# A pre-norm attention and gated-FFN block on one core: the first chunk's order, VectorE's share and the judging of batches changed in a planned schedule

## The chip, the cores and the metric

The kernel runs on one core of one Trainium2 chip. The metric is the device time of one execution in microseconds (us). A core has five engines that run side by side and wait for each other through semaphores: PE (TensorE, matrix products; its weight loads are listed apart as PEld), DVE (VectorE), ACT (ScalarE), POOL (GpSimd) and SP (SyncE, which here only issues DMA transfers). Each engine takes its own instructions in the order in which the program has them. Matrix products are written to PSUM, a small memory of eight banks of 2 KB for each of 128 partitions; everything else lives in SBUF.

## The reference

A transformer block on one sequence of 2048 tokens of 512 features, in bf16: layer norm, attention with 32 heads of 16 dimensions, a residual sum, layer norm, a gated FFN with 1792 hidden features, a second residual sum.

```python
def _A_ref(x, wqkv, wo):
    qkv = transpose(reshape(x @ wqkv, (B, S, 3, H, Dh)))     # H = 32, Dh = 16
    q, k, v = qkv[0], qkv[1], qkv[2]
    p = softmax(einsum("bhqd,bhkd->bhqk", q, k) * Dh ** -0.5)
    o = einsum("bhqk,bhkd->bhqd", p, v)
    return reshape(o, (B, S, D)) @ wo

def _B_ref(x, w_gate, w_up, w_down):
    g, u = x @ w_gate, x @ w_up
    return (sigmoid(g) * u) @ w_down

h  = x + _A_ref(layernorm(x), wqkv, wo)
h2 = h + _B_ref(layernorm(h), w_gate, w_up, w_down)
```

The costly part is the exponential of 32 x 2048 x 2048 scores.

## The kernel before, in words

**Units, tiles and groups.** Scores are computed transposed: keys on the partitions, queries along the row. A *unit* is 128 keys by 512 columns for one place `j` of four in a row of the PE array. Three units (`GU = 3`, three PSUM banks, tile `pss`) make a score tile; two such tiles fit, so the scores of tile n wait until both readers of tile n - 2 are done. There are 683 tiles, numbered in the order of their work. A *group* is 64 units. Groups with heads 0 to 7 cover a chunk of 512 queries (`(c, 0)`, `(c, 1)`); the others, `(4 + h, p)`, cover half a chunk, 256 queries of half `h`, with the eight heads of a pair `p` (1 to 3). `gseq` (L807 to 812) lists the 32 groups in their order. `(c, 0)` of all four chunks come first, then for each chunk `(c, 1)` and its six half groups. In the first chunk the halves are interleaved.

**Exponentials on two engines.** Of each score tile ACT takes two or three units in one instruction (`pt`, six buffers; L1421). In a *split* tile, one unit goes to DVE, which approximates the exponential with integer arithmetic: a linear function of the score, written as 16-bit integers and read again as bf16 (tile `J`, L1233), and three further codes that add constants to it (`code`, L1253), four units at a time. Whether tile n is split is decided in `act_step` (L1401 to 1415) by DVE's backlog and the buffers at hand. A tile that is not split is called whole here.

**Values.** PE multiplies `pt`, `J` and the codes with V (`acc`, L1207); V has a column of constants for the sums. A unit on ACT needs one such product, a unit on DVE four. At a group's end DVE transposes `acc` to `xs` (L1145) and inverts the sums, POOL scales (L1111, L1117), and DVE transposes to `ot`.

**Background work.** Everything else on PE stands in a queue `bg` of generators: V for 16 key tiles (`prep_v`, L677), K for each pair (`prep_k`, L689), Q for each chunk and pair (`prep_q`, L746), the output projection with the second layer norm's statistics (`wo_add`), the FFN's up-projections (`ffn_up`) and down-projections (`ffn_down`) for each half. Each has a due tile; `FFN_DUE` (L969) has those of the FFN. K and Q need a chain over several engines: PE projects, DVE scales (`kd` L703, `qd` L762), SP issues eight transfers that spread the rows to four places (`spread`, L194), and a shift of the exponents follows the same way (`kr` L725, `kcol` L731, `sh` L777, its transfers L780). If work that a step needs has not been done, `force` (L1017) puts it in front at once.

**The planner.** The order of each engine's instructions is written out by a planner when the program is built. It keeps a clock per engine (`T`), lets the engine that is furthest behind take the next step (`pe_step`, `act_step`, `dve_step`, `gps_step`), and places instructions by fixed costs. `pe_step` (L1323) takes scores when their two readers will be done; else it picks a batch of ready value units (`pick`, L1344) and chooses between it (`"a"`), background work (`"b"`), an idle product that keeps PE active (`fill`, L653), and waiting 40 ns. `good` (L1349) says whether a batch is full enough. `credit` grows with the rate at which background work falls due.

**Waits of the scores.** For a split tile, `dve_step` notes both readers, the exponential and DVE's first code (L1449), and `scores` (L1064) makes the first product of tile n depend on both of tile n - 2. `ex_end` is the time from which the planner thinks that the scores may start; after DVE's first code it adds 125 ns (L1447).

**The end.** After the last tile the rest of the background work, the last value products, and the FFN of the last half run one after the other.

Of the kernel before, what the change touches and what calls it, by code (L numbers as in the profile page):

```python
# [26 lines left out]
def kernel(  # L27
# [12 lines left out]
    P = 128  # L40
    S, D = A_x.shape[1], A_x.shape[2]
# [8 lines left out]
    NQC = S // QC  # L50
# [757 lines left out]
    for c in range(NQC):  # L808
        gseq += [(c, 1)]
        pairs, both = range(1, NP), (2 * c, 2 * c + 1)  # L810
        gseq += [(NQC + h, p) for h in both for p in pairs] if c else \
            [(NQC + h, p) for h, p in ((0, 1), (1, 1), (0, 2), (0, 3), (1, 2), (1, 3))]

    def chunk_of(q):
        return q if q < NQC else (q - NQC) // 2
# [150 lines left out]

    HOLD = Mark(None)
    LEAD = 12
    FFN_DUE = (256, 326, 395, 464, 533, 603, 672)  # L969
    bg = deque()  # L970
    done = {("q", 0, 0, 0), ("v0", 0)}

# [75 lines left out]
    def scores(n):  # L1048
        for k in queries(n):
            force(k)  # L1050
        pss = ps_s.tile([P, GU, QC], FP32, name="pss")
        first = True
        for a in range(2):
            for ui, (q, g, kt, j) in enumerate(tiles[n]):
                hg = head_groups(q, g)
                if a >= len(hg):
                    continue
                w = QC // len(hg)
                mm = nc.tensor.matmul(  # L1059
                    pss[:, ui, a * w:(a + 1) * w],  # L1060
                    lhsT=KT[hg[a]][32 * j:32 * j + 32, kt * P:(kt + 1) * P],
                    rhs=(QT0[q] if q < NQC and g == 0 else QT[hg[a]])[32 * j:32 * j + 32, columns(q, a)],
                    start=True, stop=True, tile_position=(32 * j, 0))
                for r in readers.get(n - 2, ()) if first else ():  # L1064
                    tc.add_manual_dep(mm.ins, r.ins.name,
                                      DependencyInfo(DependencyClass.Sync, DependencyReason.DATA),
                                      reason="both readers of the bank's last scores")
                first = False
        T["P"] = max(T["P"] + switch("s"), ex_end.get(n - 2, -LAT) + LAT, arrived(n)) + SMM
        worked(SMM * 0.25 * len(tiles[n]))  # L1070
        sc_end[n] = T["P"] + 165
        pss_n[n] = pss
# [98 lines left out]
    def av_cost(uns):  # L1171
        return MM * max(sum(un.u[3] == j for un in uns) for j in range(4))
# [147 lines left out]
    credit = 0.0  # L1320
    nxt = {"s": 0, "e": 0}

    def pe_step():  # L1323
        nonlocal credit
        t, s, e = T["P"], nxt["s"], nxt["e"]
        ready = None
        if s < N and (s < 2 or s - 2 in ex_end):
            ready = max(ex_end.get(s - 2, -LAT) + LAT, arrived(s))
            if ready <= t + 100 * (st["mode"] != "s") + 20:
                scores(s)  # L1330
                nxt["s"] += 1
                for q, p, kt, j in tiles[s]:
                    if (q, kt, j) == (NQC + NH - 1, NT - 1, 3):
                        for g in range(2 * p * (p > 1), min(2 * p + 2, FC // 2)):
                            load_pair(late_pair(g), g)
                return
        drop_read()
        last_sc = sc_end.get(e, t + 400.0)
        act_end = max(T["A"], last_sc + LAT if e < s else T["A"])
        limit = act_end + (s - e) * 905 - 520 if s < N else 1e12  # L1340
        room = limit - t
        got = [av_ready(60.0, r) for r in (1, 2, 3, 4)]
        got = [v for v in got if v and S_OUT * (st["mode"] != "a") + av_cost(v) <= room + 100]
        pick = max(got, key=lambda v: len(v) / (100 + av_cost(v))) if got else []  # L1344
        old = min((un.n for un in avq if un.held is None), default=e)
        press = e - old >= NPT - 1 or len(codes) >= CB - PRESS or len(first_codes) >= NJB or e == N
        press = press or st["cur"] < len(gseq) and lasts[gseq[st["cur"]]] < e
        last = 0 < len(pick) == av_left()
        good = pick and len(pick) * MM / 4 >= RATE * (100 + av_cost(pick))  # L1349
        group = tiles[min(e, N - 1)][-1][:2]  # L1350
        floor = -4 if not jq and T["D"] + pending() < t + 300 and lasts[group] - e < 100 else 0
        order = []
        if st["work"] == "b" and st["mode"] != "s" and credit > floor and not (press and pick):
            order.append("b")
        if last or press or good and credit < 2:
            order.append("a")
        if credit > floor:
            order.append("b")
        if good:
            order.append("a")  # L1360
        for kind in order:
            if kind == "a" and pick and av(av_cost(pick) / MM):
                return
            if kind == "b" and (2 * MM + S_OUT * (st["mode"] == "s") <= room + (0 if credit < 8 else 500)):
                used = try_bg(1e9)
                if used:
                    credit -= used
                    return
        free_pm = not st["open"] and (st["pm"] is None or st["pm"].end is not None
                                      and st["pm"].end + LAT <= t)  # L1370
        if FILL and free_pm and active(t) < FILL and MM + S_OUT * (st["mode"] == "s") <= room + FROOM:
            fill()
            return
        T["P"] = t + 40

    def act_step():
# [21 lines left out]
        taken, full = taken[len(taken) // NJ * NJ:], -(-len(taken) // NJ)  # L1398
        held_codes = len(codes) + sum(len(c.ops) for c in chains) + NCODE * full
        pick = None  # L1400
        if (len(tl) == GU and len(jq) < 2  # L1401
                and (not fresh or held_codes + NCODE <= CB and len(first_codes) + full - (len(half) > 0) < NJB)
                and max(T["D"] - start, 0.0) + 600 * len(jq) <= LATE and back <= BACK
                and len(avq) <= QMAX):
            can = [w for w in (GU - 1, 0)
                   if (fresh or tl[w][:2] == taken[0].u[:2])
                   and (back + LAST + (NJ - 1 - len(taken)) * LQ) * LS
                   <= left_in[tl[w][:2]] * 1130 + GEND]
            js = [un.u[3] for un in taken]
            good = [w for w in can if tl[w][3] not in js]  # L1410
            if good:
                pick = good[0]
            elif can and back <= EASY:
                pick = can[0]
# [20 lines left out]
    def dve_step():  # L1435
# [7 lines left out]
        if jq and sc_end[jq[0][0]] + LAT <= t + WAITJ and (half or len(first_codes) < NJB):  # L1443
            n, pss, un, ex = jq.popleft()
            first = dexp_first(pss, un)
            T["D"] = max(t, sc_end[n] + LAT) + 600
            ex_end[n] = max(un.end, T["D"] + 125)  # L1447
            tc.declare_no_dep(first.ins, ex.ins, reason="other banks of the tile")
            readers[n] = (ex, first)  # L1449
            return  # L1450
        if chains and chains[0].group == gseq[st["cur"]] and lasts[chains[0].group] < nxt["e"] + HURRY:
            pop_chain()
# [150 lines left out]
```

## Time and profile before

| | |
|---|---|
| median of 3 runs | 805.17 us (804.78 to 805.35) |
| profiled execution | 804.94 us |
| its span, first to last instruction | 803.2 us |
| mean granted clock of PE | 0.993 of full speed |
| score tiles | 683: 500 split, 182 whole, and the last with two units |

Times in rows are us from the start of the span. A row of the timeline has start, length, engine, line, operation, what it writes and reads, sizes and a count; merged rows run from the first start to the last end. In brackets stands how long the engine was idle before and what ended that. In groups (rows with two bars), the columns are busy time in us and mean duration in ns, then idle time in front. Rows of successive instructions of one engine can overlap, since a record runs from start to end and the next one may start before that end. "PEld" rows are weight loads, and "SPq" rows are the issues of transfers, not the transfers. The trace tells nothing of the planner's own clocks; where instructions stand against each other in the built program is told as "in the order".

### The profile page before, as it was taken

Reading aid. Unit: us, or ns where it says so; the run is one execution under the profiler, and the core shown is the slowest. Engines: PE = TensorE matmul, PEld = TensorE weight load, DVE = VectorE, ACT = ScalarE, POOL = GpSimd, SP = SyncE. Lnnn points to the kernel's source line nnn. Section 1 sums busy time; section 2 is a strip of 40 time slices with the busy share of each in tenths; the row PEclk is TensorE's granted clock in tenths of the full one; section 3 lists DMA queues with packets and bytes.
Section 4 is the critical chain, followed back from the end, with each engine's and each line's share of the span. In section 5 each row is a group of like instructions: output and inputs, shape, how many; then the busy total and the mean of one; then the engine's idle time right before and its main releaser. Section 6 shows DMA issues by size and latency. Waiting matters only on the chain.

```text
span 803.2 us, 34789 instructions
## 1 busy us (share of the span) xinstructions
PE 759.2 (95%) x15324; PEld 369.7 (46%) x15328; DVE 730.0 (91%) x1325; ACT 760.2 (95%) x780; POOL 52.7 (7%) x131
## 2 busy tenths in 40 slices
PE   9899998999888999999999999999999999999998
PEld 7322222443433544455445444564454446545655
DVE  7999998999979999998999998999999989999962
ACT  6999998999999999999999999999999999999962
POOL 4000000000001000100010002000100010010000
PEclk9999999999989999999999999999999999999999
DMA  6403012122400132023102220221113202322600
GB/s 194 120 2 71 2 28 61 28 66 44 151 2 22 36 102 84 10 76 100 44 16 73 77 85 11 75 82 55 36 50 97 72 29 82 108 72 79 174 28 14
DMA packets 91862, 51.32 MB, mean 64 GB/s; under 512 B 21376, under 2 KB 90624, under 8 KB 91712
## 3 DMA queue, kind: packets, MB, share of 16 engines
q1 hardware_dynamic: 91184, 49.03, 22.2%
q8 instruction: 121, 1.98, 1.0%
q14 instruction: 29, 0.24, 0.1%
q10 hardware_dynamic: 528, 0.07, 0.1%
HBM read 39.52 MB, written 2.11 MB: 52 GB/s over the span
## 4 chain that ended last, share of the span: by engine, by line
PE 38%; ACT 30%; DVE 18%; issue 10%; DMA 2%; POOL 1%; SPq 1%; DVEq 0%; ACTq 0%
ACT pt L1421 28%; PE pm L186 12%; PE acc L1207 11%; PE pss L1059 11%; DVE J L1233 8%; DVE code L1253 4%; PE gu L181 2%; ACT th L929 2%; DVE kd L703 1%; DVE xs L1145 1%; PE hp L1568 1%; DMA code<-in_A_x_dram 1%; DVE Vaug L206 1%; DMA k<-kr 1%; DVE sqk L711 0%
## 5 line engine op out<-in xcount | busy, mean ns | idle before, releaser
L1421 ACT ACTIVATE pt<-pss 128x1024 bf16<-128x1024 f32 (+1 forms) x683 | 720.1, 1174 | 11.7 <-PE pss L1059 7.2
L1233 DVE TENSOR_SCALAR J<-pss 128x512 uint16<-128x512 f32 x500 | 330.2, 676 | 22.5 <-PE pss L1059 21.3
L1059 PE MATMUL pss<-QT,KT 32*128 32x256 bf16 (+1 forms) x3584 | 269.8, 290 | 31.4 <-ACT pt L1421 20.2
L1253 DVE TENSOR_SCALAR code<-J 128x2048 uint16<-128x2048 uint16 (+2 forms) x390 | 246.5, 663 | 0.4
L1207 PE MATMUL acc<-pt,Vaug 128*17 128x256 bf16 (+1 forms) x2706 | 226.2, 292 | 1.2 <-DVE xs L1145 0.5
L1059 PEld LDWEIGHTS <-KT 32*128 32x128 bf16 x3584 | 81.7, 92 | 233.3 <-ACT pt L1421 126.4
L1207 PE MATMUL acc<-code,Vaug 128*17 128x256 bf16 (+1 forms) x2634 | 187.8, 289 | 0.2
L1207 PEld LDWEIGHTS <-Vaug 128*17 128x17 bf16 x6218 | 136.6, 90 | 96.2 <-issue 76.3
L1207 PE MATMUL acc<-J,Vaug 128*17 128x256 bf16 (+1 forms) x878 | 140.8, 291 | 0.6 <-DVE Vaug L206 0.4
L186 PE MATMUL pm<-xT,wgu 128*32 128x256 bf16 x3136 | 114.1, 274 | 0.5
L186 PEld LDWEIGHTS <-wgu 128*32 128x32 bf16 x3136 | 76.6, 96 | 25.8 <-issue 22.3
L186 PE MATMUL pm<-wd,hT 128*32 128x512 bf16 x784 | 54.8, 382 | 0.0
L1111 POOL TENSOR_TENSOR o<-xs,rec 128x256 bf16<-128x256 f32 x23 | 17.2, 747 | 421.4 <-DVE rec L1107 421.4
L913 DVE SCALAR_TENSOR_TENSOR hT<-th,pm 128x512 bf16<-128x512 f32 x49 | 32.9, 672 | 7.6 <-PE pm L186 6.8
L929 ACT ACTIVATE th<-pm 128x512 f32<-128x512 f32 x49 | 30.8, 628 | 0.2
L1145 DVE STREAM_TRANSPOSE xs<-acc 128x512 f32<-128x512 f32 x32 | 22.7, 709 | 6.4 <-PE acc L1207 6.3
L186 PEld LDWEIGHTS <-hT 128*32 128x32 bf16 x784 | 15.9, 95 | 19.7 <-issue 12.5
L186 PE MATMUL pm<-xT,wk_sb 128*32 128x512 bf16 x256 | 19.2, 383 | 0.5 <-DVE kd L703 0.5
L186 PE MATMUL pm<-xT,wq_sb 128*32 128x512 bf16 x256 | 19.3, 388 | 0.0
L1117 POOL TENSOR_TENSOR o<-xs,rec 128x256 bf16<-128x256 f32 x8 | 5.6, 705 | 190.0 <-DVE rec L1107 190.0
L186 PE MATMUL pm<-wv_sb,xT 128*32 128x448 bf16 x256 | 17.4, 356 | 0.5 <-DVE Vaug L206 0.5
L186 PE MATMUL pm<-wo_sb,ot 128*32 128x512 bf16 x224 | 16.9, 383 | 0.1
(156 smaller groups left out, 367.8 us busy)
## 6 DMA issues: line engine op xcount, KB each, us to landing
wgu<-in_B_w_gate_dram SPq DMA_DIRECT2D x49, 256.0 KB
wgu<-in_B_w_up_dram SPq DMA_DIRECT2D x49, 256.0 KB
KT<-ones SPq DMA_DIRECT2D x7, 512.0 KB
out_dram<-ob SPq DMA_DIRECT2D x15, 128.0 KB
KT<-kd SPq DMA_DIRECT2D x28, 64.0 KB
QT<-qd SPq DMA_DIRECT2D x112, 16.0 KB
wd<-in_B_w_down_dram SPq DMA_DIRECT2D x1, 1792.0 KB
xr<-in_A_x_dram SPq DMA_DIRECT2D x14, 128.0 KB
```

The costliest lines, as they stand in the source:

```text
L181: nc.tensor.matmul(ps, lhsT=lhsT, rhs=rhs, start=start, stop=stop)
L186: nc.tensor.matmul(ps[r, :], lhsT=lhsT[:, r], rhs=rhs, start=start, stop=stop, tile_position=(0, 32 * j), skip_group_check=True)
L206: nc.vector.tensor_scalar(out=Vaug[:, t, 4:H, 0:DH], in0=ps[:, 0:D - 64].rearrange("p (h d) -> p h d", d=DH), scalar1=rstd[:, t:t + 1], sc ...
L913: nc.vector.scalar_tensor_tensor(out=hT[:, 2 * k:2 * k + 2, :].rearrange("p f q -> p (f q)"), in0=th[:], scalar=1.0, in1=ps, op0=ALU.add, ...
L929: nc.scalar.activation(out=th[:], in_=ps, func=ACT.Tanh, scale=0.5)
L1059: mm = nc.tensor.matmul(pss[:, ui, a * w:(a + 1) * w], lhsT=KT[hg[a]][32 * j:32 * j + 32, kt * P:(kt + 1) * P], rhs=(QT0[q] if q < NQC and ...
L1111: V.tensor_tensor(out=o2[:, 0:NB, :].rearrange("p b (a d) -> p a b d", a=2), in0=xs[:, :, 0:DH].rearrange("p (a b) d -> p a b d", a=2), in ...
L1145: j = st["acc"] = dve(630, lambda: nc.vector.transpose(out=xs[:].rearrange("p b r -> p (b r)"), in_=acc[:]), Mark(T["P"]))
L1207: nc.tensor.matmul(acc[32 * j:32 * j + VW, a * w:(a + 1) * w], lhsT=Vaug[:, kt, 4 * hg[a] + j, :], rhs=un.ap[:, a * w:(a + 1) * w], start= ...
L1233: first = nc.vector.tensor_scalar(out=J[:, k, :], in0=src, scalar1=128 * SC * LOG2E, scalar2=float(CODE_BASE), op0=ALU.mult, op1=ALU.add)
L1253: nc.vector.tensor_scalar(out=c, in0=j, scalar1=CODE_STEP[i], scalar2=None, op0=ALU.add)
L1421: ex = nc.scalar.activation(out=pt[:, lo:lo + wa, :], in_=pss[:, lo:lo + wa, :], func=ACT.Exp, scale=SC)
```

## The change

Six edits:

- In the first chunk, `gseq` takes half 0's three pairs and then half 1's, as in the other chunks.
- The FFN's due tiles begin at 220 instead of 256 and end at 672 as before, evenly spaced.
- In tiles 30 to 139, every third tile may not be split.
- A batch of value units is judged without the 100 ns for a change of the array's mode, unless PE comes from scores; and where PE would otherwise only wait, it takes a batch that is at least 40% full if the next background work isn't ready before the batch is over (`bg_ready` is new).
- The scores of tile n carry a dependence on DVE's first code of tile n - 2 alone; that on the exponential is left to the buffer's own tracking, which puts it on the first product.
- The planner lets the scores start 50 ns after its end of DVE's first code, instead of 125.

```diff
     for c in range(NQC):
         gseq += [(c, 1)]
         pairs, both = range(1, NP), (2 * c, 2 * c + 1)
-        gseq += [(NQC + h, p) for h in both for p in pairs] if c else \
-            [(NQC + h, p) for h, p in ((0, 1), (1, 1), (0, 2), (0, 3), (1, 2), (1, 3))]
+        gseq += [(NQC + h, p) for h in both for p in pairs]
...
-    FFN_DUE = (256, 326, 395, 464, 533, 603, 672)
+    FFN_DUE = (220, 295, 371, 446, 521, 597, 672)
...
-                for r in readers.get(n - 2, ()) if first else ():
-                    tc.add_manual_dep(mm.ins, r.ins.name,
+                if first and n - 2 in readers:
+                    tc.add_manual_dep(mm.ins, readers[n - 2].ins.name,
                                       DependencyInfo(DependencyClass.Sync, DependencyReason.DATA),
-                                      reason="both readers of the bank's last scores")
+                                      reason="VectorE's reading of the bank's last scores")
...
+    def bg_ready():
+        if not bg or bg[0][2] is None or credit <= -4:
+            return 1e12
+        ends = [d.end for d in bg[0][2][2] if d is not None]
+        return T["P"] + 300 if None in ends else max(ends, default=-LAT) + LAT
...
-        pick = max(got, key=lambda v: len(v) / (100 + av_cost(v))) if got else []
+        pick = max(got, key=lambda v: len(v) / (100 * (st["mode"] == "s") + av_cost(v))) if got else []
...
-        good = pick and len(pick) * MM / 4 >= RATE * (100 + av_cost(pick))
+        good = pick and len(pick) * MM / 4 >= RATE * (100 * (st["mode"] == "s") + av_cost(pick))
...
+        if pick and len(pick) * MM / 4 >= .4 * av_cost(pick) and bg_ready() >= t + 1 * (S_OUT * (st["mode"] != "a") + av_cost(pick)):
+            if av(av_cost(pick) / MM):
+                return
         T["P"] = t + 40
...
-        if (len(tl) == GU and len(jq) < 2
+        if (len(tl) == GU and len(jq) < 2 and not (30 <= n < 140 and n % 3 == 0)
...
-            ex_end[n] = max(un.end, T["D"] + 125)
+            ex_end[n] = max(un.end, T["D"] + 50)
             tc.declare_no_dep(first.ins, ex.ins, reason="other banks of the tile")
-            readers[n] = (ex, first)
+            readers[n] = first
```

## The prediction

> **What bounds the kernel now.** I read the page's engine totals and its chain first, then busy time in six equal stretches of attention (110 tiles each, the last 102) with the stretch before them, then the exponentials by form, then the waits and the timeline where ScalarE stood still.
>
> ```profile
> span 803.2 us, 34789 instructions
> PE 759.2 (95%) x15324; PEld 369.7 (46%) x15328; DVE 730.0 (91%) x1325; ACT 760.2 (95%) x780; POOL 52.7 (7%) x131
> ACT pt L1421 28%; PE pm L186 12%; PE acc L1207 11%; PE pss L1059 11%; DVE J L1233 8%; DVE code L1253 4%; PE gu L181 2%; ACT th L929 2%; DVE kd L703 1%; DVE xs L1145 1%; PE hp L1568 1%; DMA code<-in_A_x_dram 1%; DVE Vaug L206 1%; DMA k<-kr 1%; DVE sqk L711 0%
> L929 ACT ACTIVATE th<-pm 128x512 f32<-128x512 f32 x49 | 30.8, 628 | 0.2
> ```
>
> The totals show PE and ACT level, and ACT's exponentials are the chain's largest entry with 28%; the shares alone decide nothing. The stretches do (columns: length, then busy time of PE, PE's weight loads, DVE, ACT, POOL, each with its instructions, then the granted clock and two DMA columns):
>
> ```profile
> 22.20:54.20 32.00, 28.61 (x335) 10.64 (x334) 31.62 (x61) 31.98 (x31) 0.62 (x1) 1.00 0.30 76
> 54.20:175.80 121.60, 112.35 (x1682) 38.35 (x1675) 116.46 (x214) 116.61 (x112) 3.43 (x5) 1.00 0.20 42
> 175.80:295.30 119.50, 109.25 (x2117) 49.30 (x2111) 111.22 (x197) 115.97 (x116) 8.04 (x16) 0.96 0.20 54
> 295.30:415.50 120.20, 117.13 (x2707) 58.39 (x2695) 109.63 (x194) 119.53 (x121) 9.73 (x25) 1.00 0.21 61
> 415.50:536.50 121.00, 116.25 (x2654) 60.26 (x2655) 112.52 (x201) 120.59 (x123) 7.09 (x15) 1.00 0.22 63
> 536.50:655.60 119.10, 116.57 (x2516) 55.79 (x2516) 112.07 (x197) 118.78 (x121) 8.78 (x25) 1.00 0.20 58
> 655.60:769.60 114.00, 110.79 (x2800) 62.37 (x2795) 107.17 (x189) 112.62 (x117) 6.95 (x15) 1.00 0.33 94
> ```
>
> ACT leaves 0.7, 0.4, 0.3 and 1.4 us uncovered in the last four stretches, but 5.0 and 3.5 us in the second and third row, where DVE (116.46 of 121.60) or the clock (0.96) comes in. ACT is the bound; the others matter where they make it late. What one exponential costs, by form and as unbroken runs of five and of four:
>
> ```profile
> L1421 ACT ACTIVATE pt<-pss 128x1024 bf16<-128x1024 f32 x501 | 485.4, 1062 | 10.3 <-PE pss L1059 6.3 <-PE acc L1207 2.9
> L1421 ACT ACTIVATE pt<-pss 128x1536 bf16<-128x1536 f32 x182 | 260.1, 1483 | 1.3 <-PE pss L1059 0.9
> 90.50 4.73 ACT L1421 ACTIVATE pt<-pss 128x1024 bf16<-128x1024 f32 x5
> 38.53 5.48 ACT L1421 ACTIVATE pt<-pss 128x1536 bf16<-128x1536 f32 x4
> ```
>
> A split tile (two units on ACT, one on DVE) comes every (4.73 - 1.06) / 4 = 0.91 us, a whole one every (5.48 - 1.48) / 3 = 1.33: a unit given back to ACT costs 0.42 us. In a run the records overlap by 1.06 - 0.91 = 0.15. At these paces 500 splits, 182 wholes and 49 tanh (30.8) fill 455.0 + 242.1 + 30.8 = 728 of the 747.4 us from 22.2 to 769.6; so ACT is late by about 19 us in all, some 7.6 of it in 54.2 to 175.8 (121.6 - 77 x 0.91 - 33 x 1.33). That is what the change can win.
>
> **The change, part by part.** Sums are against the profiled execution (804.94 us, its span and 1.7 around it), which is 0.2 below the median 805.17. What the planner makes of the edits stands in the order of the two built programs; counts "in the order" are from there.
>
> *Fewer units on VectorE.* In the order 485 tiles are split instead of 500; 12 of the 15 lie in tiles 30 to 139 (45 wholes for 33). ACT gets 15 x 0.42 = **+6.3 us**, on the path. DVE loses 15 first codes, and PE 60 of 6218 value matmuls; both are off the path.
>
> *Halves one by one, and other batches.* Three single places where ACT stood still, each with its cause:
>
> ```profile
> 120.22 4.20 ACT L1421 ACTIVATE pt<-pss 128x1024 bf16<-128x1024 f32 x4 [1.48 <-PE acc L1207]
> 139.42 0.69 DVE L206 TENSOR_SCALAR Vaug<-pm,rstd 128x448 bf16<-128x448 f32 x1 [1.04 <-PE pm L186]
> 140.16 0.11 PEld L1207 LDWEIGHTS <-Vaug 128*17 128x17 bf16 x7 [0.64 <-DVE Vaug L206]
> 141.35 1.02 ACT L1421 ACTIVATE pt<-pss 128x1024 bf16<-128x1024 f32 x1 [1.77 <-PE pss L1059]
> 261.22 1.02 ACT L1421 ACTIVATE pt<-pss 128x1024 bf16<-128x1024 f32 x1 [1.45 <-PE acc L1207]
> ```
>
> At 120.22 and 261.22 the exponential waits for value matmuls that still read its six-deep output buffer: in the order tiles 85 and 213 are last read seven score tiles later. After the change no tile is read later than six, and one at six. At 141.35 PE had to make V tiles 13 to 15 in front of the scores, since the value matmuls already wanted them (the last V step stands at tile 107, and the first of the three is wanted at 105); in the new order the last one stands at tile 100. With the lost overlap the three come to 1.48 + 1.77 + 1.45 + 3 x 0.15 = **-5.2 us**. What is late next at these places is the ordinary lateness, which stays in the sum.
>
> The clock: the last of these three and one more stretch lie where it was halved.
>
> ```profile
> 229.00:231.00 2.00, 1.15 (x24) 0.51 (x18) 0.69 (x1) 2.00 (x3) 0.00 (x0) 1.00 0.04 8
> 231.00:233.00 2.00, 0.92 (x18) 0.24 (x13) 1.42 (x3) 2.00 (x3) 0.00 (x0) 0.89 0.00 0
> 232.50:239.40 6.90, 6.39 (x84) 2.10 (x84) 5.94 (x11) 5.87 (x7) 0.62 (x1) 0.51 0.00 0
> 259.80:263.30 3.50, 3.31 (x56) 1.63 (x60) 3.27 (x8) 2.08 (x3) 0.62 (x1) 0.51 0.02 5
> 113.94 1.07 PE L186 MATMUL pm<-xT,wq_sb 128*32 128x512 bf16 x16
> ```
>
> PE was 46 to 58% busy in the 4 us before 232.5; then ACT lost 1.0 us uncovered, some 1.5 with the overlap. Four 512-column matmuls side by side take (1.07 - 0.38) / 3 = 0.23 us at most (last row); counted at 0.22, the thinnest four tiles of PE work in the order hold 0.27 of ACT's time (tiles 191 to 194, just there) and 0.32 (215, 216, the second episode); after the change the thinnest is 0.35, since half 0 ends at tile 170 instead of 191 and its FFN fills the gap from tile 179 on instead of 207. I take **-1.5 us**; the ends are -1.5 and +3 (two new episodes). The Trainium skill ("TensorE: Matmul & The Clock Gate", Part 1) says that the clock halves after an idle window of about 3.4 us. By that rule nothing in either order halves it, and -1.5 stands; the trace disagrees, as half-busy was enough.
>
> Batches are judged without the 0.1 us for a change of mode unless PE comes from scores, and one is taken in place of idling. In the order 146 stretches between score groups hold four or more rounds of matmuls instead of 174 (16% fewer), and 16 are empty instead of 34, though PE changes its array mode 48 times more. Of the 19 us, 19 - 6.7 = 12.3 remain; 16% of that is **-2.0 us**, between 0 and -4.
>
> *The third wait.* Now 485 score groups begin with a wait instruction for DVE, then a weight load that waits for ACT; after, the load waits for DVE and the first matmul for ACT, and no separate wait instruction is left.
>
> ```profile
> PE pss L1059 <- DVE J L1233: 6.1, 18, 0.9
> 454.11 0.68 DVE L1233 TENSOR_SCALAR J<-pss 128x512 uint16<-128x512 f32 x1
> 454.91 0.13 PEld L1059 LDWEIGHTS <-KT 32*128 32x128 bf16 x3 [0.50 <-ACT pt L1421]
> 454.94 0.39 PE L1059 MATMUL pss<-QT,KT 32*128 32x512 bf16 x3 [0.23 <-DVE J L1233]
> 118.98 0.71 DVE L1145 STREAM_TRANSPOSE xs<-acc 128x512 f32<-128x512 f32 x1
> 119.74 0.38 PE L1207 MATMUL acc<-pt,Vaug 128*17 128x512 bf16 x1 [0.53 <-DVE xs L1145]
> ```
>
> J ends at 454.79 and the matmul starts 0.15 later; a PE instruction with a DVE wait of its own starts 0.05 after it (119.69 to 119.74). So J lets the scores go 0.10 sooner, on 18 waits: -1.8. The planner now counts on it (release 0.75 us after J's start instead of 0.83). If the wait instruction was not the cause, PE stands 0.08 longer before those scores: +1.4. The xs row is the nearest of the same engine, so I take **-1.5**. Who queues behind: everything on PE.
>
> *Moved steps.* Pairs 2 and 3 are needed at tiles 128 and 149 instead of 149 and 170. Their K chain on SP before:
>
> ```profile
> 153.08 0.68 DVE L703 TENSOR_TENSOR kd<-pm,RK 128x512 bf16<-128x512 f32 x1
> 153.79 5.62 SPq L198 DMA_DIRECT2D KT<-kd  x8
> 159.51 2.70 SPq L728 DMA_DIRECT2D k<-kr  x4
> 163.31 0.14 DVE L731 TENSOR_REDUCE kcol<-k 8x1 f32<-8x4 f32 x1 [0.68 <-DMA k<-kr]
> 167.37 1.14 SPq L780 DMA_DIRECT2D QT<-sh  x2
> ```
>
> From kd's end (153.76) to the last of 22 issues (168.51) 14.75 us, and 1.1 for a landing (162.21 to 163.31): 15.9. In the new order kd's last piece stands at tiles 111 and 132, 15 to 16 exponentials before the scores that need it, which is 16.1 to 17.5 us at the paces above. It just fits; before, 30 us lay between. I put **+0.5**, up to +2.4 if both come a microsecond late. The FFN's first weight loads queue on SP behind the last of these issues, as before, at tile 143 instead of 158. POOL's normalisations move with their groups; its rows are 7% busy. The new FFN due times only shift background work, counted in the batches.
>
> *The end.* One up-projection more is left after the last scores: 32 matmuls at 114.1 / 3136 = 0.036 us, **+1.0** with its DVE step covered by the down-projection behind it.
>
> ```profile
> L186 PE MATMUL pm<-xT,wgu 128*32 128x256 bf16 x3136 | 114.1, 274 | 0.5
> ```
>
> Sum: 6.3 - 5.2 - 1.5 - 2.0 - 1.5 + 0.5 + 1.0 = -2.4: 802.5 for a profiled run, **802.7** against the median.
>
> **Rivals.** *The lateness comes back elsewhere* (slower). ACT hands two score buffers to PE, and any order has tiles where PE comes late; if the named stalls are only replaced by others, ACT's 6.3 and the end's 1.0 remain: 812. It decides from where less than 6.2 of the 10.2 us is recovered (then over +1.6). For it: three named stalls of four are one-offs of an order, and the new order was laid out with the same costs. Against: no V step is forced and no buffer is read at seven.
>
> *Two new half-clock episodes or both landings late* (no change): +3 or +2, about 805. The skill's rule speaks against the episodes, the row at 231 for them: the new order has lows of 0.35 to 0.37 at tiles 42, 85, 139 and 321.
>
> *A larger gain*: if DVE, 96% covered in the second row and relieved there of 11 first codes, and the 18 fewer empty stretches take another 4 us of the remaining 10, it is 798.
>
> **How the numbers follow.** 0.2% (1.6 us) is about what a measurement can tell here. Forecast, 800 to 803.5: 0.36; larger gain, below 800: 0.18; no change: 0.18; slower, 807 to 812: 0.28. So faster 0.54, same 0.18, slower 0.28. The range, 797.5 to 810, leaves out the far ends of the larger gain and of the returned lateness; the forecast's own is 800 to 804.
>
> **What would show it.** ACT's long forms go to 197 and the stretch of tiles 30 to 139 to about 114.1 + 5.0 plus 2 to 4 us of lateness; no ACT wait over 1 us for PE's acc or after a Vaug wait; clock 1.00 through attention; scores 0.05 instead of 0.15 after J's end; PE's waits for J below 6.1. Wrong if ACT's uncovered time stays near 12 us, if PE waits for QT's landing at tiles 128 or 149, or if a stretch with a clock of 0.5 appears near tiles 139 or 321.

## The result, and the profile after

| | before | after |
|---|---|---|
| median of 4 runs each | 805.13 us (804.78 to 805.35) | 800.82 us (799.42 to 801.79) |
| ratio, 95% interval | | 0.9951 (0.9935 to 0.9967) |
| profiled execution / its span | 804.94 / 803.2 us | 799.42 / 797.6 us |
| mean granted clock, profiled execution | 0.993 | 1.000 |
| split / whole tiles | 500 / 182 | 485 / 197 |

The change makes the kernel 0.5% faster: 4.3 us by the medians, 5.5 by the profiled executions. After's profiled execution is the fastest of its four, 1.4 us under their median, so what its trace shows is the change at its best. The page's totals and its chain, after:

```profile
span 797.6 us, 34183 instructions
PE 761.8 (96%) x15263; PEld 378.5 (47%) x15267; DVE 717.1 (90%) x1313; ACT 762.9 (96%) x780; POOL 50.2 (6%) x131
ACT pt L1429 37%; PE pm L186 11%; PE acc L1206 10%; PE pss L1058 10%; DVE J L1232 4%; DVE code L1252 2%; PE gu L181 2%; ACT th L928 1%; PE hp L1576 1%; PE pm L661 1%; DMA code<-in_A_x_dram 1%; DVE xs L1144 1%; DVE sh L777 0%; DVE qd L762 0%; DVE hT L912 0%
```

In the chain, ACT's exponentials go from 28% to 37%, and DVE's `J` and `code` from 12% to 6%: the bounding engine now follows itself more often. The same stretches after (stretch, length, busy time of PE, PEld, DVE, ACT and POOL with counts, granted clock, two DMA columns):

```profile
21.70:54.20 32.50, 29.61 (x340) 11.14 (x338) 32.20 (x61) 32.30 (x30) 0.62 (x1) 1.00 0.29 74
54.20:176.10 121.90, 113.67 (x1658) 41.32 (x1655) 109.17 (x206) 120.81 (x111) 3.41 (x6) 1.00 0.23 46
176.10:293.00 116.90, 111.32 (x2288) 55.33 (x2287) 109.88 (x194) 116.76 (x118) 6.21 (x15) 1.00 0.24 69
293.00:411.30 118.30, 115.01 (x2553) 56.78 (x2545) 110.29 (x199) 118.25 (x119) 9.73 (x25) 1.00 0.16 46
411.30:531.50 120.20, 117.69 (x2663) 61.52 (x2655) 111.65 (x198) 120.05 (x124) 6.21 (x15) 1.00 0.22 65
531.50:650.30 118.80, 116.09 (x2472) 56.34 (x2467) 110.93 (x198) 118.72 (x120) 9.97 (x25) 1.00 0.19 55
650.30:762.70 112.40, 110.47 (x2743) 61.70 (x2744) 103.31 (x185) 111.84 (x117) 6.00 (x15) 1.00 0.33 95
762.70:797.60 34.90, 29.25 (x310) 18.91 (x306) 12.26 (x23) 10.41 (x17) 0.00 (x0) 1.00 0.08 24
```

ACT's uncovered time from the first to the last exponential falls from 11.3 to 2.3 us. The second row is as long as before with 12 more whole tiles in it (121.90 for 121.60); the third is 2.6 us shorter, and its clock is 1.00 instead of 0.96; DVE leaves 12.7 us free in the second row instead of 5.1. The exponentials by form, the exponentials' one remaining row in ACT's waits, and the two rows of PE's waits that concern the score buffers (total us, times, longest):

```profile
L1429 ACT ACTIVATE pt<-pss 128x1024 bf16<-128x1024 f32 x486 | 473.6, 1078 | 1.7 <-PE pss L1058 1.2
L1429 ACT ACTIVATE pt<-pss 128x1536 bf16<-128x1536 f32 x197 | 285.5, 1497 | 0.8 <-PE pss L1058 0.5
```

```profile
ACT pt L1429 <- PE pss L1058: 1.7, 5, 0.5
PE pss L1058 <- ACT pt L1429: 18.7, 64, 1.5
PE pss L1058 <- DVE J L1232: 1.1, 3, 0.6
```

Idle time in front of the split exponentials falls from 10.3 to 1.7 us. The wait for `acc` is gone, and no exponential waits over 0.6 us.

**Where the 5.5 us went.** Idle time misses what the overlap of records hides. So I take from the trace, for every exponential, the distance to the start of ACT's next instruction less the pace at which they follow each other unhindered (the median of that distance), 0.905 us after a split tile and 1.331 after a whole one, and call it lateness:

| profiled execution | span | wholes | lateness (tiles 30-139 alone) | from last exponential to the end | stretches at half clock |
|---|---|---|---|---|---|
| before | 803.2 | 182 | 29.1 (8.0) | 32.5 | 6.8, 3.4 |
| after | 797.6 | 197 | 16.3 (3.2) | 33.8 | none |

15 wholes x 0.426 = +6.4, lateness -12.8, the end +1.3, the first exponential 0.4 earlier: -5.5. The single largest lateness left is 0.73 us. Sorted by what the late scores had waited for (ACT, where they start within 0.06 us of its exponential's end; `J`, where they start within 0.15 us, after the change 0.06, of its end; else other work or waits of PE), scores that came late because PE was at other work fell from 18.3 to 11.7 us, those held by DVE's `J` from 6.9 to 1.5.

### The profile page after: what moved, and what is told of

Read it like the earlier page. It is cut to its first block, busy times and chain, and to the rows that moved or that the text cites. A ratio compares the mean times of both kernels' runs of the same rounds, so it can differ in the third digit from the quotient of the medians.

```text
span 797.6 us, 34183 instructions
## 1 busy us (share of the span) xinstructions
PE 761.8 (96%) x15263; PEld 378.5 (47%) x15267; DVE 717.1 (90%) x1313; ACT 762.9 (96%) x780; POOL 50.2 (6%) x131
## 4 chain that ended last, share of the span: by engine, by line
ACT 39%; PE 36%; issue 14%; DVE 9%; DMA 1%; SPq 1%; ACTq 0%; DVEq 0%
ACT pt L1429 37%; PE pm L186 11%; PE acc L1206 10%; PE pss L1058 10%; DVE J L1232 4%; DVE code L1252 2%; PE gu L181 2%; ACT th L928 1%; PE hp L1576 1%; PE pm L661 1%; DMA code<-in_A_x_dram 1%; DVE xs L1144 1%; DVE sh L777 0%; DVE qd L762 0%; DVE hT L912 0%
## 5 line engine op out<-in xcount | busy, mean ns | idle before, releaser
L1232 DVE TENSOR_SCALAR J<-pss 128x512 uint16<-128x512 f32 x485 | 321.5, 680 | 23.2 <-PE pss L1058 22.3
L1252 DVE TENSOR_SCALAR code<-J 128x2048 uint16<-128x2048 uint16 (+3 forms) x393 | 241.3, 647 | 0.7
L1206 PE MATMUL acc<-pt,Vaug 128*17 128x256 bf16 (+1 forms) x2726 | 234.3, 290 | 0.8 <-DVE xs L1144 0.8
L1058 PEld LDWEIGHTS <-KT 32*128 32x128 bf16 x3584 | 92.3, 92 | 215.8 <-issue 123.7
L1206 PE MATMUL acc<-code,Vaug 128*17 128x256 bf16 (+1 forms) x2574 | 185.9, 287 | 0.0
L186 PE MATMUL pm<-xT,wgu 128*32 128x256 bf16 x3136 | 116.4, 274 | 0.9 <-DVE hT L912 0.2
```

Source lines behind the costliest of these rows:

```text
L186: nc.tensor.matmul(ps[r, :], lhsT=lhsT[:, r], rhs=rhs, start=start, stop=stop, tile_position=(0, 32 * j), skip_group_check=True)
L1058: mm = nc.tensor.matmul(pss[:, ui, a * w:(a + 1) * w], lhsT=KT[hg[a]][32 * j:32 * j + 32, kt * P:(kt + 1) * P], rhs=(QT0[q] if q < NQC and ...
L1206: nc.tensor.matmul(acc[32 * j:32 * j + VW, a * w:(a + 1) * w], lhsT=Vaug[:, kt, 4 * hg[a] + j, :], rhs=un.ap[:, a * w:(a + 1) * w], start= ...
L1232: first = nc.vector.tensor_scalar(out=J[:, k, :], in0=src, scalar1=128 * SC * LOG2E, scalar2=float(CODE_BASE), op0=ALU.mult, op1=ALU.add)
L1252: nc.vector.tensor_scalar(out=c, in0=j, scalar1=CODE_STEP[i], scalar2=None, op0=ALU.add)
```

## The experiments

The theory was that of the prediction: ACT bounds, units given back cost 0.42 us each, and the order, the batches and the wait win more than that. The rivals: the clock alone explains the gain; one edit has it all and the rest is neutral; DVE's relief, which the prediction put off the path, is worth something. Each run was made on one of three chips; ratios are against runs of the kernel before on the same chip (medians 804.51, 804.99 and 804.62 us), so compare ratios rather than medians.

| run | median us | ratio (95%) | median clock | wholes | lateness | end |
|---|---|---|---|---|---|---|
| b_wait | 803.09 | 0.998 (0.9965 to 0.9995) | 0.994 | 182 | 28.2 | 32.6 |
| b_waitc | 811.82 | 1.0095 (1.0077 to 1.0112) | 0.997 | 182 | 28.6 | 44.2 |
| b_split | 803.09 | 0.9978 (0.9967 to 0.9989) | 0.9945 | 193 | 20.8 | 32.8 |
| b_order | 821.71 | 1.021 (1.0189 to 1.0232) | 0.988 | 180 | 45.3 | 36.1 |
| a_wait | 801.2 | 0.9958 (0.9942 to 0.9973) | 0.999 | 197 | 18.0 | 33.8 |
| a_split | 818.52 | 1.0164 (1.014 to 1.0189) | 0.984 | 187 | 39.8 | 33.8 |
| a_order | 802.46 | 0.9967 (0.9953 to 0.9982) | 0.9965 | 195 | 19.4 | 33.8 |
| a_batch | 804.33 | 0.999 (0.9975 to 1.0006) | 0.9975 | 190 | 23.0 | 37.4 |
| b_keep | 805.54 | 1.0005 (0.9995 to 1.0016) | 1.000 | 182 | 30.4 | 32.5 |
| a_keep | 803.69 | 0.9982 (0.9973 to 0.999) | 0.999 | 197 | 20.8 | 33.8 |
| a_115 | 801.19 | 0.9947 (0.9934 to 0.9961) | 1.000 | 195 | 19.1 | 33.9 |
| a_fill | 805.75 | 1.0012 (0.9999 to 1.0025) | 0.999 | 190 | 23.3 | 37.3 |

The last three columns are from each run's profiled execution, whose clock is not always the median's: it was 1.000 in b_split, 0.996 in a_batch and 0.997 in a_fill. A lateness with half clock in it is larger for that reason too.

### The third wait, alone and undone

b_wait takes the edit to the wait alone into the kernel before; the order of the instructions stays the same.

```diff
-                for r in readers.get(n - 2, ()) if first else ():
-                    tc.add_manual_dep(mm.ins, r.ins.name,
+                if first and n - 2 in readers:
+                    tc.add_manual_dep(mm.ins, readers[n - 2].ins.name,
...
-            readers[n] = (ex, first)
+            readers[n] = first
```

> The kernel before with the third wait alone taken away; every engine's order stays as before. Theory (the wait instruction delays the release by VectorE): the first score matmul starts 0.06 us after the end of VectorE's first code where that comes last, instead of 0.15; 15 to 20 such places make ScalarE late, so 1.5 us less, 803.6, between 802 and 805. The three named stalls stay (1.5, 1.8 and 1.4 us). Rival (the wait is the whole gain): 800.8, as the changed kernel. Rival (the wait instruction is hidden): 805.1, and the 0.15 stays.

a_wait puts both readers back into the changed kernel (the same diff turned round).

> The changed kernel with the third wait put back and its order kept to the instruction. Theory: VectorE's release goes from 0.06 back to 0.15 us after its first code, and since this order has scores stand 0.08 us earlier it is met more often than before, at 25 to 60 places: 2 to 4 us more, 803.5. Rival (the wait is hidden): 800.8. Rival (the wait is the whole gain): 805.

The timeline of a_wait at one tile, then of after at the same tile and at another:

```profile
579.47 0.65 DVE L1232 TENSOR_SCALAR J<-pss 128x512 uint16<-128x512 f32 x1
580.23 0.13 PEld L1058 LDWEIGHTS <-KT 32*128 32x128 bf16 x4 [0.98 <-ACT pt L1429]
580.26 0.29 PE L1058 MATMUL pss<-QT,KT 32*128 32x256 bf16 x3 [0.73 <-DVE J L1232]
```

```profile
578.15 1.25 DVE L1232 TENSOR_SCALAR J<-pss 128x512 uint16<-128x512 f32 x2
578.85 0.12 PEld L1058 LDWEIGHTS <-KT 32*128 32x128 bf16 x6 [0.92 <-DVE J L1232]
578.86 0.28 PE L1058 MATMUL pss<-QT,KT 32*128 32x256 bf16 x3 [0.64 <-DVE J L1232]
...
589.35 0.67 DVE L1232 TENSOR_SCALAR J<-pss 128x512 uint16<-128x512 f32 x1
590.08 0.12 PEld L1058 LDWEIGHTS <-KT 32*128 32x128 bf16 x6 [0.26 <-DVE J L1232]
590.08 0.28 PE L1058 MATMUL pss<-QT,KT 32*128 32x256 bf16 x3
```

With two readers the scores start 0.14 us after `J`'s end (580.12 to 580.26); with one 0.06 (590.02 to 590.08). Over all tiles the least distance is 0.145 before, 0.057 in b_wait and after, 0.146 in a_wait: the separate wait instruction is the cause, as the prediction took it. The traces have 494 such instructions at the scores before, 11 after. What it is worth is another matter. In the same order it gives b_wait 0.2% (about 1.6 us, interval 0.4 to 2.8), near the -1.5 of the prediction, but PE's waits for `J` do not fall:

```profile
PE pss L1059 <- DVE J L1233: 6.4, 16, 1.2
```

Before, they were 6.1 in 18. Undone in the changed kernel, the edit costs 0.0007 of the ratio, some 0.6 us, which cannot be told from nothing; the 2 to 4 us expected there were a miss. Not for the number of places: 43 score tiles of a_wait start 0.144 to 0.147 us after a `J`'s end, within the 25 to 60 expected (54 before; 40 in b_wait and 20 in after start 0.056 to 0.059 after one). But 43 x 0.09 us on PE left ACT only 1.7 us later (lateness 18.0 for 16.3): most of what PE loses there falls into slack.

### The planner's constant

b_waitc adds to b_wait the 50 for 125 ns that the planner counts.

```diff
-            ex_end[n] = max(un.end, T["D"] + 125)
+            ex_end[n] = max(un.end, T["D"] + 50)
```

> The kernel before without the third wait, and the planner told so (50 for 125 ns). In the order: 182 whole tiles as before, 153 long batches instead of 174, V tiles 13 to 15 still forced, two tiles still read seven later (85 and 362). Theory: the wait's 1.5 us and 12% of the 12 us of ordinary lateness, 1.5: 802.1, with two of the three named stalls still there. Rival (the wait and its constant are the whole gain): 800.8. Rival (the planner's constant does nothing): as the run without it.

8.7 us slower than b_wait by the medians, where 802.1 was expected, with the same lateness. It is in the end, which is 11.6 us longer. The last stretch of b_waitc and two groups of its instructions there, then the last stretch of the kernel before:

```profile
767.20:811.80 44.60, 35.30 (x488) 24.25 (x485) 14.38 (x26) 12.26 (x20) 0.00 (x0) 1.00 0.14 43
L186 PE MATMUL pm<-xT,wgu 128*32 128x256 bf16 x192 | 6.3, 273 | 4.7 <-DVE hT L913 2.6 <-ACT th L929 2.1
L929 ACT ACTIVATE th<-pm 128x512 f32<-128x512 f32 x3 | 1.8, 597 | 7.0 <-PE pm L186 7.0
```

```profile
769.60:803.20 33.60, 28.68 (x297) 18.60 (x288) 11.67 (x23) 10.31 (x17) 0.00 (x0) 0.99 0.08 25
```

192 up-projection matmuls are left after the last exponential; in the kernel before none is, and in after 8. 6.3 us of it is PE's work, and 4.7 are waits, as the up-projections, ACT's tanh and DVE's product have no exponentials left to run beside. So one constant, changed by 75 ns, made the planner push background work out of attention. In the changed kernel the constant has the same value and the end is 33.8: there the other edits keep the work inside. The constant was not undone by itself in the changed kernel.

### Fewer units on VectorE, alone and undone

b_split takes the rule into the kernel before; a_split takes it out of the changed one.

```diff
-        if (len(tl) == GU and len(jq) < 2
+        if (len(tl) == GU and len(jq) < 2 and not (30 <= n < 140 and n % 3 == 0)
```

> The kernel before with every third tile from 30 to 139 kept whole, and nothing else. In the order: 193 whole tiles instead of 182, V no longer forced, tiles 149 and 213 read seven later. Theory: 11 x 0.42 = 4.6 us more work for ScalarE, less the V stall of 1.9, and one of two late reads moved but not gone: 807.8, slower, between 806 and 809. Rival (VectorE was the bound from 54 to 176 us, so that its relief is the gain): 802 or less.

> The changed kernel without the rule for tiles 30 to 139. In the order: 187 whole tiles instead of 197, V tiles 12 to 15 and the queries of pairs 2 and 3 forced, tiles 43 and 85 read seven later, lowest PE share 0.23. Theory: 4.2 us less work for ScalarE, but two forced query chains of 5 us or more each, one V stall of 2 and two late reads of 1.6: 810 or more. Rival (whole tiles only cost time): 796.6.

b_split's second and third stretch:

```profile
53.40:174.00 120.60, 112.30 (x1633) 38.92 (x1626) 107.19 (x203) 120.56 (x112) 3.11 (x5) 1.00 0.20 42
174.00:291.10 117.10, 104.27 (x2113) 48.98 (x2117) 112.11 (x198) 114.78 (x116) 7.08 (x16) 1.00 0.20 55
```

The rule makes the old order 0.2% faster although it gives ACT 11 units (4.7 us) more; 807.8, slower, was expected, and the rival's 802 or less was not quite reached. DVE is 107.19 us busy in the first row instead of 116.46, ACT is covered to 0.04 us, and lateness in tiles 30 to 139 falls from 8.0 to 1.9. Of these 6.1 us, the V tiles that no longer have to be forced and tile 85's late reader, 1.77 + 1.48 + 2 x 0.15, are 3.6 (in b_split no V is forced, and the tiles read seven later are 149 and 213); the other 2.5 is 0.7 at one place (124.99 us in the kernel before) and the rest in places under 0.5 us. DVE's relief may have brought it, but not through scores that waited for `J`: apart from the V stall those make 0.3 us of lateness here in the kernel before and 0.2 in b_split. DVE's relief, the fewer value products of PE and the changed order come together in this run, and no run separates them.

In the new order the rule is no matter of 2 us. Without it, in a_split, PE's waits and its timeline show:

```profile
PE pss L1058 <- DMA QT<-sh: 13.2, 3, 7.3
```

```profile
170.87 1.32 PE L1058 MATMUL pss<-QT,KT 32*128 32x256 bf16 x12 [7.26 <-DMA QT<-sh]
```

```profile
54.10:186.70 132.60, 117.46 (x1656) 41.39 (x1653) 114.64 (x212) 117.36 (x112) 3.37 (x6) 0.94 0.18 38
```

The scores of the next pair stand at the head of PE's queue and wait 7.3 us for the last transfer of its Q. In this order the planner forces Q of pairs 2 and 3 and V tiles 12 to 15 just in front of their use; with the rule it forces nothing. The stretch is 10.7 us longer, and its clock is 0.94.

### The order of the halves, alone and undone

b_order takes `gseq` and `FFN_DUE` into the kernel before; a_order gives the changed kernel the old ones.

```diff
-        gseq += [(NQC + h, p) for h in both for p in pairs] if c else \
-            [(NQC + h, p) for h, p in ((0, 1), (1, 1), (0, 2), (0, 3), (1, 2), (1, 3))]
+        gseq += [(NQC + h, p) for h in both for p in pairs]
...
-    FFN_DUE = (256, 326, 395, 464, 533, 603, 672)
+    FFN_DUE = (220, 295, 371, 446, 521, 597, 672)
```

> The kernel before with the first chunk's halves one by one and the new FFN due times alone. In the order: 180 whole tiles, V tiles 13 to 15 forced, and the queries of pairs 2 and 3 forced at tiles 128 and 149. Theory: each forced pair stops the scores until its chain over SP has landed, some 15 us less what was begun, so 5 us or more each: 815 or more, the only edit that costs time by itself. Rival (the FFN fills the thin stretch at tiles 143 to 207, and the half clock goes): 803.

> The changed kernel with the first chunk's old order and the old FFN due times. In the order: 195 whole tiles, 149 long batches, no tile read later than six, nothing forced, lowest PE share 0.36. Theory: nothing that the stalls hang on comes back, two units less for ScalarE: 800 to 801.5, the same; the order then only matters together with the other edits. Rival (the FFN's earlier start is what keeps PE even and the clock up): 803 or more, with a stretch at half clock.

Alone the order costs 17 us, by the same mechanism as a_split. ACT's and PE's waits of b_order:

```profile
ACT pt L1420 <- PE pss L1058: 22.8, 24, 7.1
```

```profile
PE pss L1058 <- DMA QT<-sh: 13.0, 3, 7.4
```

Undone in the changed kernel it costs 1.3 us by the ratios, with intervals that overlap, and the median clock is 0.9965 where after's four runs have 0.997 to 1.000. The 802.46 lies above the 800 to 801.5 expected and under the rival's 803, but the rival's stretch at half clock is there: 3.4 us from 164.8 in the profiled execution. So order and rule are one step: the order by itself is far worse, the rule by itself worth 0.2%, and what the order adds to the rest is small. `gseq` and `FFN_DUE` were not tried apart.

### The batches

a_batch judges batches in the changed kernel as before and takes none in place of idling.

```diff
-        pick = max(got, key=lambda v: len(v) / (100 * (st["mode"] == "s") + av_cost(v))) if got else []
+        pick = max(got, key=lambda v: len(v) / (100 + av_cost(v))) if got else []
...
-        good = pick and len(pick) * MM / 4 >= RATE * (100 * (st["mode"] == "s") + av_cost(pick))
+        good = pick and len(pick) * MM / 4 >= RATE * (100 + av_cost(pick))
...
-        if pick and len(pick) * MM / 4 >= .4 * av_cost(pick) and bg_ready() >= t + 1 * (S_OUT * (st["mode"] != "a") + av_cost(pick)):
-            if av(av_cost(pick) / MM):
-                return
```

> The changed kernel with the old judging of value batches. In the order: 190 whole tiles instead of 197, 165 long batches instead of 146, 36 empty stretches instead of 19, nothing forced, none read later than six. Theory: 7 x 0.42 = 2.9 us less work for ScalarE, and 13% more of the long batches' lateness of 10 us, 1.3: 799.2, a little faster. Rival (long batches and idle stretches are what makes ScalarE late): 803 or more.

Nearly the whole gain is gone; 799.2 was expected, a little faster than the changed kernel, and the rival was right. Lateness is 23.0 for 16.3, and of it scores late behind other PE work make 17.5 for 11.7: almost the 18.3 of the kernel before. This execution (805.95) has 6.8 us at half clock, though, and after's has none; a_batch's four runs at a clock of 1.000 take 802.7 to 803.9. The end is 3.6 longer, since 64 up-projection matmuls are left after the last exponential instead of 8; 7 fewer wholes take 3.0 back. By the ratios, 3.1 us in all, so some 2.5 of it is lateness. Of the edits whose undoing leaves the rest of the order on time, this one is worth most. It was not taken alone into the kernel before, so whether it would win as much without the others is not shown. The up-projections' group in the end of a_batch:

```profile
L186 PE MATMUL pm<-xT,wgu 128*32 128x256 bf16 x64 | 2.1, 273 | 1.6 <-DVE hT L912 0.9 <-ACT th L928 0.7
```

### The clock

b_keep and a_keep issue the score products of tiles with little other PE work (56 in the old order, 71 in the new) twice, to keep PE busy there; the second issue writes the same values.

```diff
+    THIN = {...}
...
-        for a in range(2):
+        for a in (0, 1) * (1 + (n in THIN)):
```

> The kernel before with each score matmul issued twice in 56 tiles (the same values to the same place) where PE has least to do beside ScalarE; all other engines' orders as before. Theory (the half clock costs 0.3 to 0.45 us for each 0.001 of the mean granted clock): the clock goes from a median of 0.993 to 0.998 or more, and the time from 804.8 to 802.5 or less, with nothing else changed. Rival (the half clock falls into slack): the clock rises and the time stays at 804.8, or grows by the 56 x 0.22 us that PE has to do in addition.

> The changed kernel with its scores twice in 71 thin tiles. Theory: its clock is at 0.997 to 1.0 already, so 0.5 us at most from the clock (800.3), less what the longer score groups cost where they make ScalarE late. Rival (PE's work is the bound in the changed kernel): 802 or more.

b_keep did raise the clock of the kernel before to 1.000, but the time stayed, where 802.5 or less was expected:

```profile
core 0: 803.6 us, clock 1.000
```

a_keep, at after's clock, shows what the doubling costs: 2.5 us by the ratios, 0.035 a tile, so some 2.0 for b_keep's 56, which is only 0.4 slower than before. By that estimate the higher clock gave back 1.6; the intervals of the three ratios leave some 0 to 3. The other view is of runs of one kernel. 78 runs of the kernel before, on the three chips, sorted by mean granted clock:

| clock | 0.989 | 0.991 | 0.992 | 0.993 | 0.994 | 0.995 | 0.996 | 0.997 | 0.998 |
|---|---|---|---|---|---|---|---|---|---|
| runs | 3 | 19 | 4 | 23 | 4 | 14 | 6 | 1 | 4 |
| mean us | 807.2 | 806.1 | 805.9 | 804.6 | 805.1 | 803.7 | 804.4 | 803.3 | 803.4 |

A line through them falls by 0.44 us per 0.001 of mean clock (0.32 to 0.51 on the chips by themselves) and stands at 801.9 us at 1.000, which none of these runs reached. After's four runs are 799.42 and 800.1 at 1.000, 801.53 at 0.998 and 801.79 at 0.997. By the line some 2.6 of the 4.3 us go with the clock (0.993 to 0.999 by the medians). At 0.998 and 0.997, which both kernels reach, after is 1.8 and 1.5 us faster, at 1.000 it is 1.8 to 2.5 under the line. So the clock alone does not explain the gain. Between 1.6 and 2.6 for its share the runs don't decide, and the line shows what goes together, not what causes it.

### Two attempts at a better version

a_115 ends the rule at tile 115; a_fill raises `FILL`, the constant that sets the planner's idle products.

```diff
-        if (len(tl) == GU and len(jq) < 2 and not (30 <= n < 140 and n % 3 == 0)
+        if (len(tl) == GU and len(jq) < 2 and not (30 <= n < 115 and n % 3 == 0)
```

> The changed kernel with its rule for whole tiles ending at tile 114 instead of 139. In the order: 195 whole tiles instead of 197, 142 long batches instead of 146, nothing forced, no tile read later than six. Theory (a whole tile costs ScalarE 0.42 us, a long batch some 0.25): 1 to 1.5 us less, 799.5. Rival (VectorE needs the relief up to tile 140): 802 or more, with VectorE's first codes late from tile 115 on.

```diff
-    FILL = 2000.0
+    FILL = 2400.0
```

> The changed kernel with the planner's idle products asked for below 2400 instead of 2000 ns of PE work in 3413. In the order: 190 whole tiles instead of 197, 149 long batches, 9 empty stretches instead of 19, 1 us more of PE work after the last scores. Theory: 2.9 us less for ScalarE, clock at 1.0, 1 to 1.5 us more at the end: 799. Rival (idle products delay real work, so ScalarE is late more often): 802 or more.

a_115 cannot be told from after, nor does it show the 799.5 expected: two wholes fewer, 2.8 us more lateness. It shows how narrow the margin of the landings is. PE's waits in a_115, two rows that after does not have:

```profile
PE pss L1058 <- DMA QT<-sh: 1.3, 4, 0.4
...
PE pss L1058 <- DMA k<-kr: 0.7, 2, 0.4
```

a_fill lost the gain, where 799 was expected: 23.3 us of lateness, an end of 37.3 with 64 up-projection matmuls as in a_batch, and a profiled clock just under full:

```profile
core 0: 804.4 us, clock 0.997
```

In these profiled executions more wholes and less lateness go together, and both count: 0.426 x wholes + lateness is 106.6 before, 100.2 after, 103.0 in b_split, 103.9 in a_batch, 104.2 in a_fill, 102.2 in a_115. a_batch has seven wholes fewer (3.0 us) and 6.7 more of lateness, part of it with the clock halved. None of the runs is clearly faster than the changed kernel.

## Why the prediction was right

The time (802.7, measured 800.82) and the sign came out, and the working held in its larger terms; several of the smaller ones did not. The gain forecast was 2.4 us, the measured one 4.3 by the medians and 5.5 by the profiled executions. Of lateness, 10.2 us were to be won and 12.8 were.

*The level.* "Late by about 19 us" was too low: counted by starts it is 29.1. The split pace of 0.91 for 0.905 makes some 2.5 of the difference, and the tanh counted at their full records (0.63) instead of what they advance ACT (0.48) some 7. The printed division gives 0.92, not 0.91: it takes off a mean record of 1.06, where the last record of that run is 1.12, and (4.73 - 1.12) / 4 is 0.90. So there was more to win than the prediction allowed. It expected to win 54% of 19 us, and 44% of 29.1 was won; that the two errors work against each other is luck.

*Fewer units, +6.3 on the path.* Right: 15 x 0.426 = 6.4, long forms 197, the stretch of tiles 30 to 139 at 121.9 where 121.1 to 123.1 was forecast. In doubt is the clause that DVE's loss of 15 codes is "off the path". b_split shows a net gain of 1.8 us by the ratio, where by that clause only the removed stalls, 3.6 us, stood against 4.7; what made the difference is not shown. The step also missed what the rule does for the planner: without it the new order forces Q and V.

*Three stalls, -5.2.* Right in kind: none of the three is left, ACT's wait for `acc` went from 2.9 us to nothing, and no exponential waits over 0.6. What was called late next, "the ordinary lateness", shrank too.

*The clock, -1.5.* Right in sign, though that too is an estimate. Its size is 1.6 by a_keep's price, 2.6 by the line through the runs with the medians, and 3.1 with the profiled executions (0.007). The step priced one execution's two stretches by ACT's idle time there; the runs of the kernel before have clocks from 0.989 to 0.998. The rule weighed beside it, of the Trainium skill ("TensorE: Matmul & The Clock Gate", Part 1), asks for an idle window of 3.4 us. The stretches at half clock were 3.4, 6.8 and 10.2 us long in these runs, which agrees with its window of 3413 ns. But PE was busy for 58 and 69% of the 3.4 us ahead of the two stretches of the kernel before, so, as the prediction read from the first of them, no idle window was needed. A busy share is no threshold either: after has 3.4 us in which PE is 49% busy, and the clock stays. The two rows of before, then that of after:

```profile
229.10:232.50 3.40, 1.97 (x36) 0.73 (x30) 1.62 (x3) 3.40 (x5) 0.00 (x0) 1.00 0.02 5
256.40:259.80 3.40, 2.36 (x34) 1.14 (x34) 3.09 (x7) 3.37 (x4) 0.20 (x1) 1.00 0.00 0
...
153.80:157.20 3.40, 1.67 (x37) 0.82 (x38) 3.09 (x7) 3.33 (x4) 0.00 (x0) 1.00 0.08 19
```

The prediction's shares of PE work in the order (0.27 and 0.32 before, 0.35 after) don't decide it alone: a_order's lowest share is 0.36, and its profiled execution was halved for 3.4 us. What decides it stays open. The same page of the Trainium skill, under "A second HAM failure mode: psum-queue depth-cycling", tells of a kernel in which frequent short idle times between groups of matmuls throttled the clock; that is nearer to the rows, and the prediction didn't weigh it.

*Long batches, -2.0.* Near. Undone alone, the edit costs 3.1 us by the ratios: more lateness and an end 3.6 us longer, less the 3.0 that fewer wholes return. That leaves some 2.5 us of lateness, within the ends put at it, 0 to -4. The profiled executions show 6.7, but a_batch's has a stretch at half clock in it. That the old judging also moves up-projections behind the last exponential was not foreseen.

*Third wait, -1.5.* The mechanism (release 0.05 instead of 0.15) is shown, at 0.057 for 0.145. The size is right in the old order (b_wait) and not in the new one (a_wait, about 0.6 and not told from zero). That PE's waits for `J` fell to 1.1 us, as forecast, is not due to it: they are 1.7 in a_wait and 6.4 in b_wait. "The planner now counts on it" was costed at nothing by itself; b_waitc shows that this line, added to b_wait, costs 8.7 us in the old order.

*Moved steps, +0.5, up to +2.4.* No score product of after waits for a landing, so 0. "It just fits" is borne out by a_115, where waits for landings take 2.0 us.

*The end, +1.0.* Measured 1.3 (32 x 0.036 is 1.2, not 1.0). The DVE step that was to be "covered by the down-projection behind it" is not. In the last stretch of before and of after, the down-projections' group reads:

```profile
L186 PE MATMUL pm<-wd,hT 128*32 128x512 bf16 x112 | 6.4, 379 | 0.0
```

```profile
L186 PE MATMUL pm<-wd,hT 128*32 128x512 bf16 x112 | 6.4, 380 | 0.9 <-DVE hT L912 0.9
```

PE waits 0.9 us for DVE's product.

*The rivals.* That lateness comes back elsewhere did not happen, but it is what b_order and a_split do, at a price (17 us) well over the 812 put on it. Of the larger gain's reasons, DVE's relief is not shown by itself, and the fewer empty stretches are a part of what a_batch undoes. The profiled execution, 799.42, lies in its range; the median does not.

What stays open: how much of the gain the clock carries (1.6 to 3.1 us by these estimates), what decides whether the clock is halved, and how much of b_split's gain is DVE's relief itself.

## What to carry to other kernels

Where two engines share the work of a bounding stage, count lateness from start to start on the bounding engine, and price a unit moved by what it saves in lateness elsewhere, not by its own length alone. Edits to an order that a planner writes are not additive: look at each first for work that it forces in front of its users and for what it leaves after the last bounding instruction, as both cost more than any of the intended gains here. An instruction that waits for two engines may get a separate wait instruction; here that made the release 0.09 us later. What such a delay costs depends on the slack behind it: about 1.6 us in the old order, 0.6 and not told from nothing in the new.

## What the runs showed of the hardware

- A separate wait instruction in front of a weight load and matmul delays their start after DVE's end from 0.057 to 0.145 us (b_wait and after, before and a_wait). The release by ACT takes 0.050 to 0.056 either way.
- The clock was halved in whole multiples of 3.4 us, and not only when PE stood idle: in the kernel before PE was 58 and 69% busy in the 3.4 us ahead, while after kept its clock through 3.4 us at 49%. The same program had mean clocks from 0.989 to 0.998 in 78 runs, and its time fell by 0.44 us per 0.001.
- Waiting for a transfer can halve PE's clock: in a_split, where PE waited 7.3 and 5.7 us for the landing of Q, and in b_order (7.4 and 5.4), a stretch of 10.2 us at half clock began in each of these waits.
- Doubling a tile's score products where PE has little other work costs some 0.035 us a tile (an estimate: a_keep's 2.5 us over 71 tiles).
